# Attention feeding a mixture of experts: three steps instead of four between scores and values, and another order of the last slot

## The chip, the cores and the metric

The kernel runs on one core of a Trainium2 chip. The metric is the device time of one launch in microseconds (us), measured for the whole program. A profiled execution gives the trace that is quoted below; its times are counted from the start of its span. Engines are named as in the profile: PE is TensorE (PEld its weight loads), DVE is VectorE, ACT is ScalarE, POOL is GpSimd, SP is SyncE, which here only issues DMAs. Each engine runs its instructions in the order in which the program gives them to it.

## The reference

Inputs are `q`, `k`, `v` of 8 batches x 8 heads x 576 positions x 64, and `phi` of 8 x 8 x 576 x 32. Two stages follow one another, all in float32:

```
a    = softmax(phi, over the 32 memories)
k_m  = einsum('bhsm,bhsd->bhmd', a, k);  v_m likewise with v
x    = softmax(q @ k_m^T / 8) @ v_m              # per head, 32 scores a position
x    = x as 4608 tokens x 512
e    = argmax(x @ w_gate), gate = softmax(...)[e], eom = sigmoid(x @ w_output_gate)[e]
out  = gate * eom * (relu(x @ w1[e]) @ w2[e])    # 8 experts, 512 -> 1024 -> 512
```

So the keys and values are first condensed into 32 memories per head, every position attends to these, and each token of the result then goes through the two layers of one expert.

## The kernel before, in words

**Attention.** Batches are taken in four pairs. The positions of a pair are cut into five groups (four of 256 positions of one batch, and one of the 64 left over of both), which makes 20 groups, numbered here 0 to 19. For each pair, `memory` builds the condensed keys `kT_...` and values `ve_b` (transpositions of the softmaxed `ph`, sums over chunks `kvt` in L691, a closing matmul L697, scaling on ACT in L708, transpositions L717, copies to `kT` and `vT_b` in L722 and L723, and the small matmul L731). Each group then passes through these pieces:

- C, `scores` (L782, PE): 16 or 32 small matmuls into a PSUM tile `bpd`
- S, `shift`: a transposition out of `bpd` (L790, DVE), the row maximum (L793, DVE), its subtraction (L795, POOL)
- X, `expo`: the exponential (L799, ACT)
- D, `divide`: sum and reciprocal (L805, L807, L809, DVE), multiplication (L810, POOL)
- B, `back`: the transposition back to `aT` (L815, DVE)
- V0 and V1, `values` (L828, PE; the copy to `xo` L830, ACT); the group of leftovers has only V0. `store` then writes `xo` to the scratch tensor `xs` by a DMA on SP, and a deferred reduction `lg` (L947, DVE) collects the router's logits.

C, V0 and V1 take their `bpd` in rotation from two buffers.

**The table that orders it.** `attention` is a generator. Step t of its loop walks through the list `ORDER`, and the piece named there is done for group t minus its `LAG`. Between the pieces stand M and m (one step of `memory`) and R with a number (that many steps of the routing). After each pair `rank` computes the routing of its tokens; from the second pair on, `route_early` makes from it the expert of the first slots (`slot`) and the lists of tokens (`idx_ga`), after which POOL issues the indirect gathers `xg` (L483). While two pairs are done, routing runs at double pace.

**The opening.** Up to step `START` attention runs alone. At step `START - 1` the rest of `memory` is forced to its end. At step `START` the piece W splits the first two weight blocks into high and low halves (L521 on ACT, L522 on DVE), and after S the loop yields "open". From there the expert stage `run` leads: after each half unit of a slot it calls `hook`, which does three entries of `ORDER` and two routing steps.

**The expert stage.** The list `order` has 14 slots in the unconditional stream: ten of three blocks of 128 tokens, then four of two. `turn_x` transposes the gathered tokens (L993) and splits them into `xh` and `xl`; the first layer (L1127) multiplies each of four weight blocks in three passes (high by high, low by high, high by low), ACT and DVE make `hh` and `hl` of the result (L1132, L1133), and the second layer (L1146) goes through the weight blocks u = 4 to 7 with the blocks k of 128 tokens inside. When u is 7, `finish_y` scales a block's result on ACT (L1106) and POOL scatters it to `out` by an indirect DMA (L1107). Behind the stream stand slots of single blocks under a condition on a counted number (L1256); in the profiled execution none of them runs.

## Time and profile before

| quantity | value |
|---|---|
| median of 3 runs | 595.33 us (595.21 to 598.23) |
| the profiled execution's own time | 595.97 us |
| its span | 594.3 us |
| mean granted clock of TensorE | 0.959 |
| PE busy | 539.3 us (91%) |
| DVE, ACT, POOL busy | 340.9, 273.0, 160.7 us |
| DMA | 124.13 MB, mean 209 GB/s |

The page of the profile divides the span into 40 slices of some 15 us and gives the busy share of each engine by slice; the views of windows, of time order and of waits cut it finer. A busy PE is not a PE at its peak, and an engine's idle time counts only where others wait for it, so the shares are read by stage: attention alone up to about 115 us, the opening, the expert stage with the rest of attention between its matmuls up to about 190 us, the expert stage alone, and the end.

### The profile page before, as it was taken

Reading aid. Unit: us, or ns where it says so; the run is one execution under the profiler, and the core shown is the slowest. Engines: PE = TensorE matmul, PEld = TensorE weight load, DVE = VectorE, ACT = ScalarE, POOL = GpSimd, SP = SyncE. Lnnn points to the kernel's source line nnn. Section 1 sums busy time; section 2 is a strip of 40 time slices with the busy share of each in tenths; the row PEclk is TensorE's granted clock in tenths of the full one; section 3 lists DMA queues with packets and bytes.
Section 4 is the critical chain, followed back from the end, with each engine's and each line's share of the span. In section 5 each row is a group of like instructions: output and inputs, shape, how many; then the busy total and the mean of one; then the engine's idle time right before and its main releaser. Section 6 shows DMA issues by size and latency. Waiting matters only on the chain. (4 is left out here: it accounts for less than half of the span.)

```text
span 594.3 us, 10781 instructions
## 1 busy us (share of the span) xinstructions
PE 539.3 (91%) x4107; PEld 464.3 (78%) x4107; DVE 340.9 (57%) x686; ACT 273.0 (46%) x456; POOL 160.7 (27%) x192
## 2 busy tenths in 40 slices
PE   3788677788999999999999999999999999999980
PEld 2455455487788898998989899898989988989970
DVE  4487789677855589983544535354453526556200
ACT  4376554544445365434435444444444445555310
POOL 2244376731345036203303030130303012300100
PEclk9979879879999999999999999999999999999995
DMA  8999999974558578646646446474645538762000
GB/s 300 413 374 387 410 378 324 318 251 142 160 169 299 174 243 281 213 128 200 219 142 206 130 162 192 136 221 142 199 126 166 164 136 261 242 206 82 28 18 13
DMA packets 41276, 124.13 MB, mean 209 GB/s; under 512 B 9408, under 2 KB 9472, under 8 KB 40832
## 3 DMA queue, kind: packets, MB, share of 16 engines
q1 hardware_dynamic: 35136, 102.71, 52.2%
q0 software_dynamic: 6080, 20.65, 9.7%
q8 instruction: 34, 0.56, 0.4%
q14 instruction: 26, 0.21, 0.1%
HBM read 102.99 MB, written 20.87 MB: 208 GB/s over the span
## 5 line engine op out<-in xcount | busy, mean ns | idle before, releaser
L1127 PE MATMUL bps<-xh,whl 128*128 128x384 f32 (+1 forms) x896 | 213.8, 322 | 0.0
L1146 PE MATMUL bps<-whl,hh 128*128 128x512 f32 x608 | 203.7, 399 | 0.0
L522 DVE TENSOR_TENSOR whl<-w,whl 128x1024 fp32r<-128x1024 f32 x112 | 136.4, 1227 | 71.3 <-ACT whl L521 70.8
L1127 PEld LDWEIGHTS bps<-xh,whl 128*128 128x128 f32 x896 | 157.1, 190 | 1.4 <-issue 0.6
L1127 PE MATMUL bps<-xl,whl 128*128 128x384 f32 (+1 forms) x448 | 143.8, 321 | 0.0
L1146 PEld LDWEIGHTS bps<-whl,hh 128*128 128x128 f32 x608 | 114.2, 188 | 25.7 <-issue 2.5
L1146 PE MATMUL bps<-whl,hl 128*128 128x512 f32 x304 | 118.7, 390 | 0.0
L521 ACT CAST whl<-w 128x1024 fp32r<-128x1024 f32 x112 | 115.9, 1046 | 0.0
L1132 ACT ACTIVATE hh<-bps 128x384 fp32r<-128x384 f32 (+1 forms) x96 | 48.9, 510 | 102.0 <-PE bps L1127 97.7
L1133 DVE SCALAR_TENSOR_TENSOR hl<-bps,hh 128x384 fp32r<-128x384 f32 (+1 forms) x96 | 55.2, 576 | 58.9 <-ACT hh L1132 51.3
L1127 PEld LDWEIGHTS bps<-xl,whl 128*128 128x128 f32 x448 | 85.1, 190 | 0.5
L1107 POOL DMA_INDIRECT out<-y,idx_ol x23 | 23.1, 1003 | 213.7 <-ACT y L1106 186.4
L1146 PEld LDWEIGHTS bps<-whl,hl 128*128 128x128 f32 x304 | 57.3, 189 | 10.1
L995 DVE TENSOR_TENSOR xl<-bps,xh 128x384 fp32r<-128x384 f32 (+1 forms) x48 | 27.8, 579 | 60.7 <-ACT xh L994 60.5
L1106 ACT ACTIVATE y<-bps,xg 128x512 f32<-128x512 f32 x38 | 26.2, 689 | 68.9 <-issue 23.1
L994 ACT CAST xh<-bps 128x384 fp32r<-128x384 f32 (+1 forms) x48 | 23.9, 498 | 72.9 <-PE bps L993 71.2
L483 POOL DMA_INDIRECT xg<-xs,idx_gl x23 | 28.2, 1227 | 24.3 <-DVE idx_ol L242 17.6
L830 ACT COPY xo<-bpd 128x576 f32<-128x576 f32 x36 | 22.5, 639 | 22.5 <-PE bpd L828 13.1
L795 POOL TENSOR_TENSOR ea<-ea,mx 128x512 f32<-128x512 f32 (+1 forms) x20 | 19.2, 962 | 46.0 <-DVE mx L793 41.7
L828 PE MATMUL bpd<-ve_b,aT 64*128 64x144 f32 (+1 forms) x320 | 28.6, 327 | 2.1 <-DVE ea L790 1.9
L913 POOL TENSOR_SCALAR Aw<-iota_row,row 128x128 bf16<-128x128 bf16 x36 | 26.9, 763 | 12.4 <-DVE row L903 12.4
L993 PE MATMUL bps<-ident,xg 128*128 128x128 f32 x152 | 26.0, 286 | 2.3 <-DVE ea L790 1.8
(232 smaller groups left out, 427.1 us busy)
## 6 DMA issues: line engine op xcount, KB each, us to landing
w<-wall SPq DMA_DIRECT2D x112, 512.0 KB
kvt<-kv SPq DMA_DIRECT2D x32, 512.0 KB
xs<-xo SPq DMA_DIRECT2D x16, 576.0 KB
qt<-qT SPq DMA_DIRECT2D x16, 512.0 KB
ph<-phiT SPq DMA_DIRECT2D x3, 1152.0 KB
kv<-kv SPq DMA_DIRECT2D x4, 512.0 KB
ph<-phiT SPq DMA_DIRECT2D x4, 288.0 KB
xs<-xo SPq DMA_DIRECT2D x8, 144.0 KB
```

Source lines behind the costliest of these rows:

```text
L483: G.indirect_dma_start(out=z["xg"][:, k], out_offset=None, in_=xs[0:z["rows"]], in_offset=bass.IndirectOffsetOnAxis(ap=z["idx"][0][:, q:q ...
L521: A.copy(hl[:, 0], w[:])
L522: V.tensor_tensor(hl[:, 1], w[:], hl[:, 0].bitcast(F32), ALU.subtract)
L828: T.matmul(px[to:to + n, r, sl], z["aT"][h, o:o + n], ves[2 * bp + b][h, g], start=True, stop=True)
L913: (G if AWP else V).tensor_scalar(Aw[:, bp * NCH + c], iota_row[:], row[:, c:c + 1], None, ALU.is_equal)
L993: T.transpose(pt[:, j, k * P:(k + 1) * P], xg[:, k, o:o + P], ident[:])
L995: V.tensor_tensor(xl[:, c:c + w, 0:n], pt[:, :, 0:n], xh[:, c:c + w, 0:n].bitcast(F32), ALU.subtract)
L1106: A.activation(y[:], py, AF.Copy, scale=z["xg"][:, k, P:P + 1])
L1127: T.matmul(pb[:, j % pb.shape[1], 0:n_], w[:, b, o:o + P], x[a][:, cc, 0:n_], start=(n == 0), stop=(n == 11))
L1132: A.activation(h_[:, js, 0:n_], pb[:, :, 0:n_], AF.Relu)
L1133: V.scalar_tensor_tensor(l_[:, js, 0:n_], pb[:, :, 0:n_], 0.0, h_[:, js, 0:n_].bitcast(F32), ALU.max, ALU.subtract)
L1146: T.matmul(py[k], h[u - 4][a][:, f, k * P:(k + 1) * P], w[:, b, DM * f:DM * f + DM], start=(u == 4 and f == 0 and n == 0), stop=(u == 7 an ...
```

## The change

`ORDER` is rewritten and four numbers beside it are changed. X is now done in the step of its S (`LAG` 0 instead of 1), B one step behind S instead of two, and V two steps instead of three; D keeps its lag of one. V0 now stands behind D, X between V0 and V1, and B behind V1 near the end of the step. The list has 15 entries instead of 16 (R0, which did nothing, is gone). `START` is 16 instead of 17. In `several`, the second layer of the last slot of a stream goes through all four weight blocks for the first block of tokens and then again for the next, instead of through all blocks of tokens for each weight block; for all other slots the order of that layer is the same.

```diff
-ORDER = ["R4", "W", "X", "S", "R0", "m", "D", "M", "B", "V0", "R1", "R1", "V1", "M", "m", "C"]
-LAG = {"X": 1, "B": 2, "D": 1, "V": 3, "C": -1}
+ORDER = ["R4", "W", "S", "m", "D", "V0", "R1", "M", "X", "V1", "R1", "M", "B", "m", "C"]
+LAG = {"X": 0, "B": 1, "D": 1, "V": 2, "C": -1}
 TICK = 0
 HOOK = (3, 2)
-START = 17
+START = 16
@@ several @@
             py = [bank([DM], "ps") for _ in range(nb)]
-            for u in range(4, 8):
+
+            turns = [(u, k) for u in range(4, 8) for k in range(nb)]
+            if 8 * i + 8 == st.hi:
+                turns.sort(key=lambda t: t[1])
+            for step, (u, k) in enumerate(turns):
                 w = st.take(i, u)
-                for k in range(nb):
-                    for f in range(2):
-                        for n, (a, b) in enumerate(PASS):
-                            T.matmul(py[k], h[u - 4][a][:, f, k * P:(k + 1) * P], w[:, b, DM * f:DM * f + DM],
-                                     start=(u == 4 and f == 0 and n == 0), stop=(u == 7 and f == 1 and n == 2))
-                    if u == 7:
-                        finish_y(z, k, py[k])
-                    hook()
-                    step = nb * (u - 4) + k
-                    if step in TURN[nb]:
-                        nxt(TURN[nb].index(step))
-                st.done(PUMP[0])
+                for f in range(2):
+                    for n, (a, b) in enumerate(PASS):
+                        T.matmul(py[k], h[u - 4][a][:, f, k * P:(k + 1) * P], w[:, b, DM * f:DM * f + DM],
+                                 start=(u == 4 and f == 0 and n == 0), stop=(u == 7 and f == 1 and n == 2))
+                if u == 7:
+                    finish_y(z, k, py[k])
+                hook()
+                if step in TURN[nb]:
+                    nxt(TURN[nb].index(step))
+                if k == nb - 1:
+                    st.done(PUMP[0])
```

How the table moves instructions is seen at three places.

**POOL around the first gathers.** The three gathers `xg<-xs,idx_ga` are the first tokens of the expert stage. Before, POOL's order there is this (L795 is the subtraction of S, L810 the multiplication of D; the form 128x256 belongs to the leftover group 14):

```order
L795 TENSOR_TENSOR ea<-ea,mx 128x256
L810 TENSOR_TENSOR ea<-ea,sa 128x512
L483 DMA xg<-xs,idx_ga 128x576 x3
L795 TENSOR_TENSOR ea<-ea,mx 128x512
L810 TENSOR_TENSOR ea<-ea,sa 128x256
```

And now:

```order
L795 TENSOR_TENSOR ea<-ea,mx 128x512
L810 TENSOR_TENSOR ea<-ea,sa 128x512
L710 TENSOR_TENSOR ve_b<-kvm,hmask 128x2x128
L483 DMA xg<-xs,idx_ga 128x576 x3
L795 TENSOR_TENSOR ea<-ea,mx 128x256
L810 TENSOR_TENSOR ea<-ea,sa 128x512
```

The subtraction for group 14 stood ahead of the gathers and now stands behind them; ahead of them now stands that of group 13.

**ACT up to the opening.** Before, the last rows of ACT ahead of the expert stage are these (L722 with `kT_197` and `kT_198` are the condensed keys of the last pair's two batches, L799 the exponentials, L830 the copies of values, L708 the scaling of the memory, L521 the piece W):

```order
L722 COPY kT_197<-bpa 64x128 x2
L723 COPY vT_b<-bpa 64x256
L799 ACTIVATE ea<-ea 128x256
L830 COPY xo<-bpd 128x576 x2
L799 ACTIVATE ea<-ea 128x512
L708 ACTIVATE kvm<-pk,rs 128x128 x2
L722 COPY kT_198<-bpa 64x128 x2
L723 COPY vT_b<-bpa 64x256
L830 COPY xo<-bpd 128x576 x2
L521 CAST whl<-w 128x1024 x2
```

And now:

```order
L799 ACTIVATE ea<-ea 128x256
L830 COPY xo<-bpd 128x576
L722 COPY kT_197<-bpa 64x128 x2
L723 COPY vT_b<-bpa 64x256
L830 COPY xo<-bpd 128x576
L799 ACTIVATE ea<-ea 128x512
L830 COPY xo<-bpd 128x576
L708 ACTIVATE kvm<-pk,rs 128x128 x2
L722 COPY kT_198<-bpa 64x128 x2
L723 COPY vT_b<-bpa 64x256
L521 CAST whl<-w 128x1024 x2
```

The exponential of group 14 stood behind the copy to `kT_197` and now stands ahead of it; the exponential of group 15 now stands between the two copies of values of group 13.

**PE behind the first layer of the first slot.** L246 is the matmul that counts tokens for the next routing; it takes its operand `ohc_90` from DVE. Before:

```order
L828 MATMUL bpd<-ve_b,aT 128x144 x4
L246 LDWEIGHTS ones_b
L246 MATMUL pr<-ohc_90,ones_b 128x8
L1146 MATMUL bps<-whl,hh 128x512
L1146 MATMUL bps<-whl,hl 128x512
```

And now (L1149 is the line of before's L1146):

```order
L1149 MATMUL bps<-whl,hh 128x512 x2
L1149 MATMUL bps<-whl,hl 128x512
L1149 MATMUL bps<-whl,hh 128x512
L782 MATMUL bpd<-qt,kT_198 32x256 x8
L246 LDWEIGHTS ones_b
L246 MATMUL pr<-ohc_90,ones_b 128x8
```

Before, values stood directly ahead of L246; now six matmuls of the second layer and the scores of group 18 stand between the values and it.

## The prediction

> **What bounds the kernel now.** I read the page first (its slices), then windows of 5 us around the opening, then every engine in order of time there, and last the chain of waits.
>
> ```profile
> PE   3788677788999999999999999999999999999980
> ```
> ```profile
> 115.00:120.00 5.00, 3.67 (x51) 1.84 (x49) 3.38 (x7) 4.69 (x9) 2.15 (x3) 0.56 1.07 400
> 120.00:125.00 5.00, 4.02 (x16) 4.02 (x17) 4.03 (x8) 1.44 (x3) 2.76 (x3) 0.50 0.98 371
> ```
>
> In the slices PE has holes up to the tenth one (about 150 us) and is then full until the last two. So between the first slots and the end, only PE's own work counts, and neither edit takes a matmul away. What can move the end is when the first layer (L1127) starts, what stalls PE in the ten or twenty microseconds behind that, and what comes after the last matmul. The two windows (columns: PE, PEld, DVE, ACT, POOL busy, granted clock, DMA share, GB/s) are the opening.
>
> The end, from POOL, ACT and PE in order of time and from the chain of waits:
>
> ```profile
> 576.32 0.69 ACT L1106 ACTIVATE y<-bps,xg 128x512 f32<-128x512 f32 x1 [9.00 <-PE bps L1146]
> 577.28 0.97 POOL L1107 DMA_INDIRECT out<-y,idx_ol  x1 [17.93 <-ACT y L1106]
> 577.68 0.69 ACT L1106 ACTIVATE y<-bps,xg 128x512 f32<-128x512 f32 x1 [0.67 <-PEq L1257]
> 581.79 0.97 POOL L1107 DMA_INDIRECT out<-y,idx_ol  x1 [3.54 <-ACTq L1257]
> ```
> ```profile
> 577.28 3.74 DMA out<-y,idx_ol
> ```
>
> The second scatter of the last slot has its data at 577.68 + 0.69 = 578.37 but starts at 581.79: the chain shows that what ends last before it is the landing of the first scatter, at 577.28 + 3.74 = 581.02. Scatters to `out` go one after another.
>
> **The end of the program, costed.** Matmuls of the second layer follow one another at (576.98 - 576.30)/3 = 0.227 us:
>
> ```profile
> 576.30 0.39 PE L1146 MATMUL bps<-whl,hl 128*128 128x512 f32 x1
> 576.98 0.39 PE L1146 MATMUL bps<-whl,hl 128*128 128x512 f32 x1
> ```
>
> The last slot has two blocks of 24 such matmuls. With all of block 1 behind block 0, block 0 is complete 24 x 0.227 = 5.4 us before the end of PE instead of 1.36 us; its scatter starts at about 573.2 and lands by 577. The second then waits only for its own `y`. The first scatter started 0.27 us behind its `y` (577.01 to 577.28), which gives 578.64 and a gain of 3.15 us; with the 0.77 us that passed between release and start of the second (581.02 to 581.79) it is 2.65. I take **-3.0**. Nothing behind the last scatter changes. The weights of all four blocks must be split by then: the last L522 is long past (DVE's last start is at 552.6).
>
> ```profile
> 552.64 1.23 DVE L522 TENSOR_TENSOR whl<-w,whl 128x1024 fp32r<-128x1024 f32 x1 [0.26 <-ACT whl L521]
> ```
>
> The Trainium skill (DMA: Bandwidth & Descriptors, Anatomy of one DMA) fits a DMA issued from GpSimd as 2.0 us plus its bytes over 436 GB/s. For 256 KB that is an estimated 2.6 us, so the first scatter would have blocked only to 579.9 and the gain would be some 1.3 us. The row has 3.74 us, and it decides.
>
> **The opening, costed.** I set T at the first gather and follow the queues on both sides of it.
>
> ```profile
> 108.30 1.25 POOL L483 DMA_INDIRECT xg<-xs,idx_ga  x1 [1.40 <-DVE i L240]
> 112.18 1.06 POOL L795 TENSOR_TENSOR ea<-ea,mx 128x512 f32<-128x512 f32 x1
> 113.27 0.63 ACT L799 ACTIVATE ea<-ea 128x512 f32<-128x512 f32 x1 [3.08 <-POOL ea L795]
> 114.21 0.59 PE L717 MATMUL bpa<-ident,kvm 128*128 128x128 f32 x2 [2.40 <-ACT kvm L708]
> 114.83 0.53 ACT L722 COPY kT<-bpa 64x128 f32<-64x128 f32 x2 [0.42 <-PE bpa L717]
> 116.84 2.00 ACT L521 CAST whl<-w 128x1024 fp32r<-128x1024 f32 x2
> 120.98 2.18 PE L993 MATMUL bps<-ident,xg 128*128 128x128 f32 x9 [1.83 <-DVE ea L790]
> 122.81 0.67 PE L1127 MATMUL bps<-xh,whl 128*128 128x384 f32 x1
> ```
>
> Now: T = 108.30; three gathers hold POOL to 112.16; the exponential of group 15 waits for POOL; the memory's scaling, `kT_198` and the copies of values follow on ACT; the casts W start at T + 8.54; 5.97 us behind them comes L1127, at T + 14.51.
>
> Changed, by the order of ACT and POOL: the gathers end at T + 3.9. Behind them on POOL stands the subtraction of group 14 (0.61), on ACT its exponential (0.42), a copy of values (0.64), and only then `kT_197` (0.53): T + 6.1. The scores of group 15 need it and wait on PE; cold they take 1.11, to T + 7.2. Then S of 15 (0.71 + 0.69), its subtraction (1.05), its exponential (0.63), a copy of values (0.64) and half the scaling (0.3): T + 11.2. L717 0.59, `kT_198` 0.53, `vT_b` 0.37: the casts start at T + 12.7, and with 5.97 and one `lg` (0.3) L1127 comes at T + 19.0. That is **+4.5** from T. Durations that were not quoted yet, and the parts of S, D and B:
>
> ```profile
> 105.28 0.61 POOL L795 TENSOR_TENSOR ea<-ea,mx 128x256 f32<-128x256 f32 x1
> 106.27 0.42 ACT L799 ACTIVATE ea<-ea 128x256 f32<-128x256 f32 x1
> 116.47 1.11 PE L782 MATMUL bpd<-qt,kT 64*32 64x256 f32 x16
> 107.90 0.71 DVE L790 STREAM_TRANSPOSE ea<-bpd 128x512 f32<-128x512 f32 x1
> 108.64 0.69 DVE L793 TENSOR_REDUCE mx<-ea 128x16 f32<-128x512 f32 x1
> 114.58 0.68 DVE L805 TENSOR_REDUCE sa<-ea 128x16 f32<-128x512 f32 x1
> 115.29 0.32 DVE L807 TENSOR_TENSOR sa<-sa,eps 128x16 f32<-128x16 f32 x1
> 115.64 0.25 DVE L809 RECIPROCAL sa<-sa 128x16 f32<-128x16 f32 x1
> 144.57 0.65 DVE L815 STREAM_TRANSPOSE aT<-ea 128x512 f32<-128x512 f32 x1
> ```
>
> Its bounds: 0, if `kT_197` is copied before the gathers after all; +6, if every matmul on the way is cold.
>
> T itself comes earlier. The routing that makes the gathers' lists starts when the values of group 9 are out, and it needs as many routing steps as now. Values of group 9 move to the place where those of group 8 stand:
>
> ```profile
> 82.97 2.29 PE L828 MATMUL bpd<-ve_b,aT 64*128 64x144 f32 x16
> 88.69 0.72 PE L828 MATMUL bpd<-ve_b,aT 64*64 64x144 f32 x16
> 84.35 0.64 ACT L830 COPY xo<-bpd 128x576 f32<-128x576 f32 x1 [0.35 <-PE bpd L828]
> 89.50 0.64 ACT L830 COPY xo<-bpd 128x576 f32<-128x576 f32 x1
> ```
>
> Their copies stand 89.50 - 84.35 = 5.15 us apart, less one back transposition (0.65) that DVE must do earlier: **-4.5**. Bounds: -2.65 (if DVE alone sets the pace, what falls away before T is one S and one D, 0.71 + 0.69 + 0.68 + 0.32 + 0.25) and -5.7 (the two values, 88.69 - 82.97). So the opening's two terms cancel, with both ends at -5.7 and +3.4.
>
> In the Trainium skill (TensorE: Matmul & The Clock Gate, Part 1) an idle window of about 3.4 us halves PE's clock, and about as much work restores it. The granted clock of 0.50 from 120 us agrees. The wait for `kT_197` on PE is, by my sum, about 3 us, just under that window; by the page the scores of group 15 could be warm and the sum 0.45 less, or cold as I took them.
>
> SP's order also changes: the last two memory chunks `kvt`, 512 KB each, go out behind the first three weight blocks `w`, which SP issues ahead of T.
>
> ```profile
> w<-wall SPq DMA_DIRECT2D x112, 512.0 KB
> ```
>
> Together that is 2.6 MB, 6.4 us at the 400 GB/s of the window from 115. By my sum the chunks are used just ahead of the scaling, some 10 us behind T: covered. Without that cover, what they are late is added to the opening.
>
> **Behind the opening.** One group's scores more fall between the expert matmuls: (134.19 - 133.60) = **+0.6**.
>
> ```profile
> 133.60 0.66 PE L782 MATMUL bpd<-qt,kT 64*32 64x256 f32 x16
> 134.19 0.44 PE L1127 MATMUL bps<-xh,whl 128*128 128x384 f32 x1
> 144.99 0.76 PE L828 MATMUL bpd<-ve_b,aT 64*128 64x144 f32 x8
> 148.12 0.17 PE L246 MATMUL pr<-ohc,ones_b 128*128 128x8 bf16 x1 [2.36 <-DVE ohc L870]
> ```
> ```profile
> 142.82 0.49 ACT L1132 ACTIVATE hh<-bps 128x384 fp32r<-128x384 f32 x1 [1.44 <-PE bps L1127]
> 146.30 0.55 DVE L1133 SCALAR_TENSOR_TENSOR hl<-bps,hh 128x384 fp32r<-128x384 f32 x1
> ```
>
> L246 stalls PE by 2.36 us because DVE is late: it has `hh` at 143.31 and gets to `hl` at 146.30. In the changed order S of a group stands further ahead and one B behind L870, so about 2 us of DVE's work (0.71 + 0.69 + 0.65) leave this stretch, and L246 stands behind six more matmuls and one C (0.6). I leave a stall of 0.7: **-1.6**; bounds -2.36 and 0. The B moved there has its V0 two hooks later, which hides it.
>
> **Sum.** -3.0 + 4.5 - 4.5 + 0.6 - 1.6 = -4.0. The profiled execution took 595.97 us (span 594.3), so 592.0 for it; the median of the runs is 0.64 lower, which gives 591.3. I say **591.5**.
>
> **Rivals.**
>
> *The opening gains most of a step.* If the chain behind the gathers lengthens by 1 us and not by 4.5, the time is 588.0. For it: ACT now waits only 3.08 us for POOL there. Against it: the order on POOL and ACT, by which that wait now stands ahead of two groups' work.
>
> *The opening comes later and eats the gain of the end.* T gains only DVE's 2.65 us (1.85 less) and the chain is cold all through (+6, 1.5 more): 594.9. For it: between 95 and 100 DVE is busy 4.89 us of 5, so it may set the pace of the routing. Against it: what stands between values of group 9 and the gathers is the same work in both orders.
>
> ```profile
> 95.00:100.00 5.00, 3.62 (x81) 2.68 (x79) 4.89 (x31) 3.06 (x7) 2.33 (x4) 1.00 1.02 400
> ```
>
> *Slower: values wait for B.* Now a whole step lies between B and V0 of a group; changed, it is two hooks: 4.1 us in the first layer (twelve matmuls of 384 columns each, 0.227 x 384/512 = 0.17 us) and 2.7 in the second (six of 0.227). DVE was 143.31 to 146.30, 3 us, late. If it is later than two hooks for the six groups behind the opening, PE stalls at each V0; at 1.5 us each that is 591.5 + 9 = 600.5. It decides once DVE's lateness passes two hooks. Against it: DVE loses work in just that stretch.
>
> **How the numbers follow.** Forecast (589.5 to 593.5) 0.50; opening earlier (588) 0.20; opening later (594.9) 0.22; values stall (600.5) 0.08. A measurement of this kernel tells about 0.5% from no change, here 592.35 and 598.3. Two thirds of the forecast's chance and all of the early opening lie below: faster 0.54. The rest of the forecast and the late opening: same 0.38. Slower 0.08. The range is 587.5 to 595.5: it takes in the early and the late opening and leaves out the stalls.
>
> **What would show it.** Right: the last scatter starts 0.3 to 0.8 us behind its `y`; the first gather comes near 104 and the first L1127 near 123; `kT_197` is copied behind the gathers; L246 stalls under 1 us. Wrong: L1127 before 120 or behind 126, a V0 that waits for DVE between 125 and 190, or a last scatter that still waits for a DMA.

## The result, and the profile after

The changed kernel takes **601.66 us** (median of 6 runs, 600.02 to 603.19) beside 595.4 us for the kernel before (6 runs, 593.72 to 598.23). The ratio is 1.0101, 95% interval 1.0072 to 1.0129: the change makes it 6 us slower. The prediction was 591.5 us, range 587.5 to 595.5, with a chance of 0.08 on slower; it was wrong in direction. Among the runs of the experiments below one, of the end alone, took 952.39 us; its ratio leaves that run out, its median does not (593.54 us, without it 593.02).

The profiled execution of the changed kernel took 601.28 us, its span is 599.5 (before 595.97 and 594.3). The span divides at the same marks as the prediction's sum:

| stretch | before | after | forecast | measured |
|---|---|---|---|---|
| start to first gather (T) | 108.30 | 110.87 | -4.5 | +2.57 |
| T to first L1127 | 14.51 | 21.10 | +4.5 | +6.59 |
| first L1127 to PE's end | 454.78 | 453.42 | +0.6 - 1.6 | -1.36 |
| PE's end to the span's end | 16.71 | 14.11 | -3.0 | -2.60 |

Two of the four terms came as forecast. What is missing against the forecast lies ahead of the first L1127: 7.1 us ahead of T, and 2.1 between T and L1127.

The end, from PE, ACT and POOL of the changed kernel in order of time, and from its chain of waits:

```profile
580.03 0.69 ACT L1106 ACTIVATE y<-bps,xg 128x512 f32<-128x512 f32 x1 [4.92 <-PE bps L1149]
581.00 0.97 POOL L1107 DMA_INDIRECT out<-y,idx_ol  x1 [13.85 <-ACT y L1106]
585.00 0.39 PE L1149 MATMUL bps<-whl,hh 128*128 128x512 f32 x1
585.48 0.69 ACT L1106 ACTIVATE y<-bps,xg 128x512 f32<-128x512 f32 x1 [4.75 <-PE bps L1149]
586.93 0.97 POOL L1107 DMA_INDIRECT out<-y,idx_ol  x1 [4.96 <-ACT y L1106]
```
```profile
581.00 5.16 DMA out<-y,idx_ol
```

The second scatter now waits for its own `y` (585.48 + 0.69 = 586.17) and starts 0.76 us behind it. But the first one has only just landed: it took 5.16 us in place of the 3.74 before, to 581.00 + 5.16 = 586.16. The two waits end level, so nothing is left to gain there by an earlier `y` alone.

The opening, from POOL, ACT and PE of the changed kernel in order of time:

```profile
110.87 1.24 POOL L483 DMA_INDIRECT xg<-xs,idx_ga  x1 [1.46 <-DMA w<-wall]
115.40 0.42 ACT L799 ACTIVATE ea<-ea 128x256 f32<-128x256 f32 x1 [4.53 <-POOL ea L795]
116.24 0.54 ACT L722 COPY kT<-bpa 64x128 f32<-64x128 f32 x2
116.55 0.94 PE L782 MATMUL bpd<-qt,kT 64*32 64x256 f32 x16 [1.75 <-ACT kT L722]
121.51 0.64 ACT L830 COPY xo<-bpd 128x576 f32<-128x576 f32 x1 [4.34 <-DMA xs<-xo]
125.09 1.99 ACT L521 CAST whl<-w 128x1024 fp32r<-128x1024 f32 x2
129.53 2.79 PE L993 MATMUL bps<-ident,xg 128*128 128x128 f32 x12 [4.10 <-issue]
131.97 0.67 PE L1127 MATMUL bps<-xh,whl 128*128 128x384 f32 x1
```

`kT_197` is indeed copied behind the gathers, and the next scores wait for it. But a wait that the prediction does not have stands behind it: 4.34 us for a store (`xs<-xo`) that must land before its buffer is written again. Not all of it is loss. The scaling of the memory (L708), which comes three rows of ACT later and starts at 123.09, needs PE's sums, and PE ends them at 122.08 + 0.28 = 122.36:

```profile
122.08 0.28 PE L697 MATMUL pk<-zero 1*128 1x256 bf16 x1
```

By that the store costs the casts at most 0.73 us here, as long as PE's own row stays as it is.

What happens ahead of T shows first in one step, from the scores' transposition (S, L790) of group 9 to that of group 10. Before, from DVE, ACT and POOL:

```profile
70.24 0.43 DVE L790 STREAM_TRANSPOSE ea<-bpd 128x256 f32<-128x256 f32 x1
73.92 0.53 ACT L722 COPY kT<-bpa 64x128 f32<-64x128 f32 x2
74.86 0.42 ACT L799 ACTIVATE ea<-ea 128x256 f32<-128x256 f32 x1
75.02 5.29 POOL L913 TENSOR_SCALAR Aw<-iota_row,row 128x128 bf16<-128x128 bf16 x9 [1.33 <-DVE row L903]
75.29 0.70 DVE L790 STREAM_TRANSPOSE ea<-bpd 128x512 f32<-128x512 f32 x1
```

The same step in the changed kernel, from DVE, POOL, ACT and PE:

```profile
72.84 5.24 POOL L913 TENSOR_SCALAR Aw<-iota_row,row 128x128 bf16<-128x128 bf16 x9 [0.33 <-DVE row L903]
73.38 0.44 DVE L790 STREAM_TRANSPOSE ea<-bpd 128x256 f32<-128x256 f32 x1
78.05 0.60 POOL L795 TENSOR_TENSOR ea<-ea,mx 128x256 f32<-128x256 f32 x1
78.69 0.42 ACT L799 ACTIVATE ea<-ea 128x256 f32<-128x256 f32 x1 [3.61 <-POOL ea L795]
79.69 0.71 DVE L815 STREAM_TRANSPOSE aT<-ea 128x512 f32<-128x512 f32 x1 [3.06 <-POOL ea L810]
80.30 0.53 ACT L722 COPY kT<-bpa 64x128 f32<-64x128 f32 x2
80.60 1.38 PE L782 MATMUL bpd<-qt,kT 64*32 64x256 f32 x16 [2.58 <-ACT kT L722]
82.07 0.72 DVE L790 STREAM_TRANSPOSE ea<-bpd 128x512 f32<-128x512 f32 x1 [1.42 <-PE bpd L782]
```

In both kernels a routing gives POOL a burst of nine one-hot rows (L913), over 5 us long. Before, the exponential (L799) and `kT` of that step were all but done when it began, and S of group 10 followed 5.05 us behind that of group 9. Now the subtraction (L795) of group 9 stands behind the burst, its exponential waits in the same step, and behind that exponential on ACT stand the copies of `kT`, on which PE's next scores wait; on DVE, B (L815) waits for the multiplication behind that subtraction. The step takes 8.69 us. The waits of a whole execution, by the view of waits; before:

```profile
ACT ea L799 <- POOL ea L795: 7.1, 3, 3.1
PE bpd L782 <- ACT kT L722: 2.1, 4, 1.0
```

and changed (us in total, times, longest):

```profile
DVE aT L815 <- POOL ea L810: 17.0, 12, 4.1
ACT ea L799 <- POOL ea L795: 15.3, 11, 4.5
PE bpd L782 <- ACT kT L722: 5.1, 4, 2.6
```

B's waits for POOL are new altogether. I call the two waits the two hand-overs: an engine takes in one step what POOL makes in that same step.

One step tells too little, since a delay can move on into the next. In the kernel before, the burst shows later: an exponential waits 2.66 us for POOL at 81.36, and the step from group 11 to group 12 takes 7.5 us. So the table below has the three steps from S of group 9 to S of group 12 too: 16.4 us before (to 86.60) and 20.7 changed (to 94.11). First before, then changed:

```profile
86.60 0.72 DVE L790 STREAM_TRANSPOSE ea<-bpd 128x512 f32<-128x512 f32 x1 [0.74 <-PE bpd L782]
```
```profile
94.11 0.70 DVE L790 STREAM_TRANSPOSE ea<-bpd 128x512 f32<-128x512 f32 x1
```

### The profile page after: what moved, and what is told of

Same layout as the page of the kernel before. It is cut to its first block, busy times and chain, and to the rows that moved or that the text cites. A ratio compares the mean times of both kernels' runs of the same rounds, so it can differ in the third digit from the quotient of the medians.

```text
span 599.5 us, 10767 instructions
## 1 busy us (share of the span) xinstructions
PE 546.3 (91%) x4107; PEld 468.9 (78%) x4107; DVE 340.2 (57%) x686; ACT 271.6 (45%) x456; POOL 160.9 (27%) x192
## 5 line engine op out<-in xcount | busy, mean ns | idle before, releaser
L1127 PE MATMUL bps<-xh,whl 128*128 128x384 f32 (+1 forms) x896 | 214.1, 322 | 0.0
L1149 PE MATMUL bps<-whl,hh 128*128 128x512 f32 x608 | 203.8, 400 | 0.0
L1127 PEld LDWEIGHTS bps<-xh,whl 128*128 128x128 f32 x896 | 157.1, 190 | 1.6 <-ACT hh L1132 0.4
L1127 PE MATMUL bps<-xl,whl 128*128 128x384 f32 (+1 forms) x448 | 143.9, 321 | 0.0
L1149 PEld LDWEIGHTS bps<-whl,hh 128*128 128x128 f32 x608 | 114.3, 188 | 23.0
L1149 PE MATMUL bps<-whl,hl 128*128 128x512 f32 x304 | 118.8, 391 | 0.0
L521 ACT CAST whl<-w 128x1024 fp32r<-128x1024 f32 x112 | 115.9, 1046 | 0.0
L1127 PEld LDWEIGHTS bps<-xl,whl 128*128 128x128 f32 x448 | 85.1, 190 | 0.5
L1107 POOL DMA_INDIRECT out<-y,idx_ol x23 | 25.1, 1090 | 209.9 <-ACT y L1106 186.9
L1149 PEld LDWEIGHTS bps<-whl,hl 128*128 128x128 f32 x304 | 57.3, 189 | 10.1
L828 PE MATMUL bpd<-ve_b,aT 64*128 64x144 f32 (+1 forms) x320 | 31.5, 343 | 7.3 <-DVE aT L815 2.9
L795 POOL TENSOR_TENSOR ea<-ea,mx 128x512 f32<-128x512 f32 (+1 forms) x20 | 19.2, 961 | 69.8 <-DVE mx L793 51.9
L828 PEld LDWEIGHTS bpd<-ve_b,aT 64*128 64x128 f32 (+1 forms) x320 | 23.1, 204 | 15.8 <-issue 8.6
L830 ACT COPY xo<-bpd 128x576 f32<-128x576 f32 x36 | 22.8, 634 | 22.0 <-DMA xs<-xo 8.4
L993 PE MATMUL bps<-ident,xg 128*128 128x128 f32 x152 | 25.3, 285 | 4.1 <-issue 4.1
```

What stands on the lines that cost most here:

```text
L521: A.copy(hl[:, 0], w[:])
L828: T.matmul(px[to:to + n, r, sl], z["aT"][h, o:o + n], ves[2 * bp + b][h, g], start=True, stop=True)
L993: T.transpose(pt[:, j, k * P:(k + 1) * P], xg[:, k, o:o + P], ident[:])
L1107: G.indirect_dma_start(out=out, out_offset=bass.IndirectOffsetOnAxis(ap=z["idx"][1][:, z["q0"] + k:z["q0"] + k + 1], axis=0), in_=y[:], in ...
L1127: T.matmul(pb[:, j % pb.shape[1], 0:n_], w[:, b, o:o + P], x[a][:, cc, 0:n_], start=(n == 0), stop=(n == 11))
L1149: T.matmul(py[k], h[u - 4][a][:, f, k * P:(k + 1) * P], w[:, b, DM * f:DM * f + DM], start=(u == 4 and f == 0 and n == 0), stop=(u == 7 an ...
```

## The experiments

The runs were timed in five sets, each beside the kernel before on the same chip; its medians in the five sets lie between 595.51 and 596.48, so a difference of 1 us between kernels of two sets is no finding. The positions come from one profiled execution of each kernel, and the same order of work has its first gather at 110.87 in one kernel and 112.89 in another (the changed kernel, and the table alone), so less than 2 us between two profiles tells nothing by itself.

| kernel | time | ratio, 95% interval | S 9 to 10 | S 9 to 12 | first gather | first L1127 |
| --- | --- | --- | --- | --- | --- | --- |
| before | 595.4 |  | 5.1 | 16.4 | 108.3 | 122.8 |
| changed | 601.7 | 1.0101 (1.0072 to 1.0129) | 8.7 | 20.7 | 110.9 | 132.0 |
| end alone | 593.5 | 0.9963 (0.9945 to 0.9982) | 5.0 | 16.3 | 107.4 | 121.9 |
| table alone | 605.1 | 1.0152 (1.0131 to 1.0174) | 8.7 | 22.2 | 112.9 | 134.3 |
| opening alone | 603.4 | 1.0107 (1.0076 to 1.0138) | 5.1 | 15.9 | 107.8 | 121.3 |
| B in the next step | 624.8 | 1.0513 (1.0484 to 1.0542) | 10.0 | 25.0 | 122.7 | 146.7 |
| routing ahead of B | 602.8 | 1.0121 (1.0083 to 1.0160) | 8.9 | 21.1 | 111.0 | 132.7 |
| exponential in the next step | 599.0 | 1.0065 (1.0036 to 1.0094) | 7.2 | 20.0 | 109.3 | 130.2 |
| exponential behind the copies | 599.6 | 1.0066 (1.0051 to 1.0080) | 7.2 | 20.3 | 109.1 | 130.0 |
| multiplication on DVE | 603.6 | 1.0138 (1.0118 to 1.0157) | 9.0 | 20.7 | 112.9 | 135.1 |
| both hand-overs gone | 599.5 | 1.0062 (1.0047 to 1.0076) | 6.2 | 16.9 | 105.8 | 126.6 |
| one-hots on DVE | 597.7 | 1.0040 (1.0018 to 1.0062) | 4.8 | 16.2 | 107.8 | 128.7 |
| burst split | 598.6 | 1.0044 (1.0024 to 1.0064) | 6.3 | 17.7 | 110.1 | 130.9 |
| end and one-hots on DVE | 593.4 | 0.9961 (0.9946 to 0.9976) | 6.6 | 16.6 | 107.8 | 122.2 |
| store first | 602.3 | 1.0097 (1.0070 to 1.0123) | 8.7 | 21.4 | 111.8 | 133.1 |
| gathers later | 601.0 | 1.0094 (1.0073 to 1.0116) | 8.5 | 20.9 | 113.5 | 130.9 |
| store and gathers | 599.3 | 1.0064 (1.0041 to 1.0087) | 8.7 | 21.5 | 114.3 | 130.8 |
| these and one-hots on DVE | 596.3 | 1.0011 (0.9990 to 1.0032) | 4.8 | 16.2 | 110.8 | 128.1 |
| three mends | 598.6 | 1.0053 (1.0034 to 1.0072) | 5.4 | 16.8 | 110.5 | 125.9 |
| four mends | 597.5 | 1.0022 (1.0008 to 1.0036) | 5.4 | 16.8 | 111.7 | 126.3 |

### The change taken apart

The end alone is the kernel before with the new order of the last slot. The table alone is the changed kernel without it. The opening alone is the kernel before with

```diff
-START = 17
+START = 16
```

> The kernel before with the one edit at the end: the last slot's second layer block by block; table, lags and opening as before. Theory (the two edits add up; in the changed kernel the last scatter starts 0.76 us behind its y and 14.1 us pass from the end of PE to the end of the span, where it was 16.7): 2.65 us less than the kernel before, 592.7 beside 595.4, ratio 0.9955. Rival (the end's gain hangs on the opening, or the first scatter still blocks the second): no change, 595.4, ratio 1.000.

> The changed kernel without the edit at the end: values two steps behind scores, opening at step 16, last slot as in the kernel before. Theory (the whole loss is the table's): 601.7 + 2.65 = 604.3, ratio to the kernel before 1.015. Rival (the edit at the end costs something, the table less): 601.7 or lower, ratio 1.010 or below.

> The kernel before with START 16 alone: table and lags as before, last slot as before. Theory (an opening one step sooner costs nothing by itself; one exponential, two copies of values and one S leave the way between the gathers and the casts, some 2.5 us, and one group's scores more stand between the expert matmuls, 0.6): first gather near 108 as before, casts near 114.5, time 593 to 594.5, ratio 0.997. Rival (the sooner opening is the loss: it stretches the chain behind the gathers by 6 us as in the changed kernel): 598 to 601, ratio 1.005 to 1.010.

The end alone gives 2.2 us, the table alone costs 9.4 (605.1 against 595.7 in its set); their sum, 7.2, stands beside 6.3 for the whole change. So within the noise the edits add up, and the whole loss is the table's.

The opening alone was missed on both sides. The first L1127 comes 1.5 us earlier, as the theory had it, and the stall at L246 nearly goes (0.46 us), yet the time is 7 us longer. It is lost later. Windows of PE in that kernel (columns as in the prediction: PE, PEld, DVE, ACT, POOL, clock, DMA share, GB/s), and what PE waits for there:

```profile
190.00:195.00 5.00, 0.60 (x5) 0.18 (x1) 0.00 (x0) 0.64 (x1) 3.78 (x5) 0.73 0.93 326
194.18 0.45 PE L993 MATMUL bps<-ident,xg 128*128 128x128 f32 x1 [4.03 <-DMA xg<-xs,idx_gb]
```

The experts begin a step earlier, but the lists of the next slots (`idx_gb`) are done at 188.6, where the kernel before has them at 179.2; PE runs out of slots and waits 5.9 us in all for their gathers. I read this as the price of values that still stand three steps behind their scores; no run shows that by itself. If so, the earlier opening needs the values' earlier step, and neither half of the table can be judged alone.

### Which hand-over stretches the steps

First the two hand-overs one by one, as the first theory (B) and its rival (the exponential) had them:

```diff
 B in the next step, behind S
-ORDER = ["R4", "W", "S", "m", "D", "V0", ..., "M", "B", "m", "C"]
+ORDER = ["R4", "W", "S", "B", "m", "D", "V0", ..., "M", "m", "C"]
-LAG = {"X": 0, "B": 1, ...}
+LAG = {"X": 0, "B": 2, ...}
 exponential in the next step
-ORDER = ["R4", "W", "S", "m", ..., "M", "X", "V1", ...]
+ORDER = ["R4", "W", "X", "S", "m", ..., "M", "V1", ...]
-LAG = {"X": 0, ...}
+LAG = {"X": 1, ...}
 routing ahead of B
+ORDER = ["R4", "W", "B", "S", "m", "D", "V0", "R1", "M", "X", "V1", "R1", "M", "m", "C"]
+LAG = {"X": 0, "B": 2, ...}
```

> The changed kernel, but the back transposition (B) of a group is put into the next step, behind S and ahead of V0 of the same group; lag of the values 2, X at lag 0, opening at step 16. Theory (DVE's 11 waits for POOL's multiplication, 16.4 us up to 135 us, stretch the steps, so that the gathers start at 110.87 and not near 104): without these waits the gathers start near 104 to 106 and the time falls by 5 to 7 us, to 595 to 597. Rival (ACT's 11 waits for POOL's subtraction, 15.3 us, stretch them): DVE's waits move elsewhere, the gathers stay near 110 and the time is 600 to 602. Second rival (only the chain behind the gathers counts): the gathers come earlier, the time stays at 600 to 602.

> The changed kernel, but the exponential (X) of a group is put into the next step, ahead of S, as in the kernel before; B stays behind D of the same step, lag of the values 2, opening at step 16. Theory (DVE's waits for POOL's multiplication are the cause): DVE still waits some 16 us, and the time is 600 to 603. Rival (ACT's waits for POOL's subtraction, 15.3 us, are the cause): these waits fall away, the gathers start near 104 to 106, the time is 595 to 597.

> The changed kernel, but B of a group stands in the next step, behind the four routing steps and ahead of S; X at lag 0, values at lag 2, opening at 16. Theory (DVE's wait for POOL's multiplication at the end of each step holds up the routing that follows it and with it PE, 4.66 us at L246): DVE's waits for the multiplication before the first gather fall from 11.6 to under 6 us, PE's wait at L246 falls to 2 to 3 us, first gather 1 to 3 us earlier, time 598.5 to 601. Rival (B later makes the values wait, as in the run with B behind S): PE waits for B at the values, first gather later than 112, time over 604.

B in the next step costs 23 us more. The run does not test what it was made for: DVE's waits for POOL are gone, but with B behind S and ahead of V0 a ring closes over one step. PE's scores wait in its queue behind the values, these for B, B on DVE for S, and S for the scores (PE waits for B at V0 17 times, 37.6 us in all, 4.5 at the longest). With the routing ahead of B, DVE's waits for POOL before T fall from 11.6 to 6.1 us, just above what was expected, PE's wait at L246 from 4.66 to 3.46, and the time stays at 602.8: S waits 20.4 us for PE there, where it waited 16.9. So B's waits, where DVE shows them, are not the time that is lost; the theory of B alone falls. The exponential in the next step gains 2.7 us, half of what its theory asked, and not at the burst: from S of group 9 to S of group 12 it still takes 20.0 us.

Then the multiplication was put on DVE (B never waits for POOL), the exponential was left in its step but placed behind the copies of `kT` on ACT, and both hand-overs were taken away at once (exponential in the next step, multiplication on DVE):

```diff
 multiplication on DVE
-G.tensor_tensor(eav, eav, sa..., ALU.mult)
+V.tensor_tensor(eav, eav, sa..., ALU.mult)
 exponential behind the copies
-ORDER = [..., "R1", "M", "X", "V1", "R1", "M", "B", "m", "C"]
+ORDER = [..., "R1", "M", "V1", "R1", "M", "X", "B", "m", "C"]
```

> The changed kernel with the division's multiplication (L810) on DVE instead of POOL, so that B never waits for POOL. Theory (what costs is the hand-over to POOL and back within one step, not DVE's own work): DVE's 11.6 us of waits at B go away, some 0.7 us of work per group comes in their place, POOL's subtractions run 1 us earlier; first gather 1 to 4 us earlier than 110.9, time 597.5 to 600.5. Rival (DVE is simply full: its work sets the steps): first gather 112 to 116, time 603 to 607.

> The changed kernel with the exponential (X) of a group still in its own step, but behind that step's second memory piece, so that on ACT it stands behind the copies of kT and of the second values and not ahead of them. Theory (in the changed order an exponential that waits for POOL stands on ACT ahead of the copies of kT, on which the next scores wait on PE: 3.61 us and 2.58 us at group 9): PE's waits of scores for kT fall below 2.5 us from 5.1, S of groups 9 and 10 stand about 7 us apart and not 8.7 (B still waits there for POOL), first gather 1.5 to 3 us earlier than 110.9, time 598 to 600. Rival (B's wait for POOL holds the step just as long): S 8.5 us apart, first gather 110 or later, time 601 to 603.

> The changed kernel with the exponential in the next step ahead of S, and the division's multiplication on DVE: neither ACT nor DVE takes a result of POOL in the step that asks for it. Theory (each of the two hand-overs passes POOL's bursts on, so that one alone brings little: 2.7 us less with the exponential, 1.9 us more with the multiplication): S of groups 9 and 10 stand under 6.5 us apart, first gather at 106 to 108, time 595 to 598, in spite of 0.69 us more of DVE's work per group. Rival (DVE's own work sets the steps): first gather 110 or later, time 600 to 603.

With the multiplication on DVE the time and the first gather are the rival's, and DVE's own work may have its part in that; but the same step is 9.0 us long although B waits for nothing, and DVE itself stands idle in it. From POOL, ACT and PE of that kernel:

```profile
74.14 5.53 POOL L913 TENSOR_SCALAR Aw<-iota_row,row 128x128 bf16<-128x128 bf16 x9
80.29 0.42 ACT L799 ACTIVATE ea<-ea 128x256 f32<-128x256 f32 x1 [4.00 <-POOL ea L795]
81.90 0.53 ACT L722 COPY kT<-bpa 64x128 f32<-64x128 f32 x2
82.20 1.38 PE L782 MATMUL bpd<-qt,kT 64*32 64x256 f32 x16 [3.15 <-ACT kT L722]
```

The delay comes through the exponential and `kT`. With the exponential behind the copies that way is shut (PE's waits for `kT` fall from 5.1 to 1.6 us), and the step is still 7.2, because B waits for POOL. With both gone it is 6.2. The three steps show it more plainly: they take 20.0 and 20.3 us with the exponential's way shut, 20.7 with B's, and 16.9 only with both. The two hand-overs are two doors for one delay. In time, though, both together (599.5, between the ranges of the theory and of its rival) bring no more than the exponential alone (599.0). The multiplication adds 13 us of work to DVE (16 of 0.71 and 4 of 0.43), which may be why, but was not separated; and that kernel's profiled execution, at 596.8 us, was the fastest of its six, so its early first gather flatters it.

### The burst itself

> The changed kernel with the nine one-hot rows of a routing (Aw, L913) on DVE instead of POOL. Theory (POOL's two bursts of one-hots, 5.24 us from 72.8 and 5.67 us from 100.3, stand ahead of a subtraction and a multiplication, and DVE and ACT, which now take both in the same step, wait behind them: 3.06 us of B's wait at 79.7): S of groups 9 and 10 stand 6 us apart and not 8.7, the first gather comes 2 to 4 us earlier than 110.9, time 598 to 600. Rival (the steps are long for another reason; DVE gets nine instructions more per routing): first gather at 110 to 113, time 601 to 604.

> The changed kernel with the first routing's one-hot rows (L913 x9 on POOL) given out one by one, so that six of the nine stand behind the subtraction of group 9 and the multiplication of group 8 instead of ahead of them; no work is moved to another engine. Theory (the burst ahead of these two makes DVE wait 3.06 us at B and ACT at X in that step, and the values of group 9 and the routing behind them come later by as much): S of groups 9 and 10 stand 6 to 7 us apart and not 8.7, first gather 1.5 to 3 us earlier than 110.9, time 598.5 to 600.5. Rival (the gain with the one-hots on DVE came from the second burst, or from POOL having less to do): first gather 110 to 112, time 601 to 603.

> The kernel before with the end block by block and the one-hot rows on DVE instead of POOL; table and opening as before. It tells whether the 4 us that this gave in the changed kernel hang on the changed table. Theory (before, no engine takes POOL's results in the same step, so the bursts are covered): within 1 us of the end alone, 592.5 to 594.5. Rival (POOL's bursts cost in any order): 3 to 4 us less, 589.5 to 590.5.

The one-hots went to DVE by a switch that the kernel has; the split only lets other pieces of the step in between one-hots of the first routing:

```diff
 one-hots on DVE
-AWP = 1
+AWP = 0
 burst split
-                    if c % 3 == 2:
+                    if bp == 0 or c % 3 == 2:
                         yield
```

On DVE the one-hots bring 4.0 us. The split moves six of nine one-hots of a single burst behind the subtraction and the multiplication and takes no work from POOL; the step falls from 8.7 to 6.3, the three steps from 20.7 to 17.7 (16.2 with the one-hots on DVE), and the time by 3.1 us. From POOL and DVE of the split kernel:

```profile
75.36 1.78 POOL L913 TENSOR_SCALAR Aw<-iota_row,row 128x128 bf16<-128x128 bf16 x3 [0.33 <-DVE row L903]
75.90 0.44 DVE L790 STREAM_TRANSPOSE ea<-bpd 128x256 f32<-128x256 f32 x1
77.11 0.61 POOL L795 TENSOR_TENSOR ea<-ea,mx 128x256 f32<-128x256 f32 x1
78.12 1.05 POOL L810 TENSOR_TENSOR ea<-ea,sa 128x512 f32<-128x512 f32 x1 [0.40 <-DVE sa L809]
82.15 0.72 DVE L790 STREAM_TRANSPOSE ea<-bpd 128x512 f32<-128x512 f32 x1 [1.97 <-PE bpd L782]
```

Its first gather came only 0.8 us earlier and not 1.5 to 3, since S of groups 8 and 9 was already 2.5 us later in that execution than in the changed kernel's, ahead of the burst. In the table of before the one-hots on DVE bring nothing (593.4 beside 593.5 for the end alone). So the burst costs what it costs only because the changed table takes POOL's results in the step that makes them. This is shown by time and by the steps; the split was not run in the old table.

### The chain behind the gathers

> The changed kernel, but SP issues the first three weight blocks behind the two memory chunks and the store of the values of group 11, not ahead of them; every engine's own order is the same. Theory (that store is issued at 110.69 behind 2.6 MB and lands at 121.4; ACT waits 4.34 us for its buffer at the values of group 13, with the scaling of the memory and the casts behind it): the wait falls below 1 us, the casts start 3 to 4 us earlier behind the first gather (10 to 11 us, not 14.2), time 597.5 to 599.5. Rival (what comes next holds the chain, so the wait only moves): casts still 13 us or more behind the first gather, time 600.5 to 602.5.

> The changed kernel, but the three first gathers stand on POOL behind the subtraction of group 14 and the multiplication of group 13 and not ahead of them. Theory (the gathers hold POOL 3.9 us ahead of the chain subtraction, exponential, kT_197, scores, casts, while their own data has 8 us of slack before the casts are through): the gathers start 1.5 to 2 us later, but the casts 2.5 to 3.9 us earlier (121.2 to 122.6 in place of 125.1), time 598 to 599.5. Rival (something else, the store's buffer or the memory's last chunks, ends last in that chain): casts within 1 us of 125, time 600.5 to 602.5.

> The changed kernel with both orders changed that alone moved little: the store of group 11's values ahead of the first weight blocks on SP, and the first gathers behind the subtraction of group 14 and the multiplication of group 13 on POOL. Theory (two waits end at nearly the same time in the chain behind the gathers, the store's buffer at 120.5 and the subtraction's chain at 120.2, so only both together shorten it): casts at 120.5 to 122 in place of 125.1, first L1127 near 128, time 597.5 to 599. Rival (a third wait, the memory's last chunks, holds the casts): casts at 123.5 or later, time 600 to 602.

> The same as the run with store and gathers, and the one-hots on DVE. Theory (the bursts delay the first gather, the two orders shorten the chain behind it; the two add up): 4 us below the run with store and gathers, 593.5 to 595, so the changed table with these three comes level with the kernel before or just below it, but not below the end alone (593.5). Rival (the chain is then held by the memory, which no mend moves): 597 to 598, as with the one-hots alone.

The first run holds back the fetch of the first weight blocks, so that SP issues memory chunks and store ahead of them; the second holds back the gathers on POOL:

```diff
 store first
-                stream.fetch()
+                defer("wf", stream.fetch)    # LATE["wf"] = 10
 gathers later
-                gathers(0)
+                defer("ga", lambda: gathers(0))    # LATE["ga"] = 5
```

On SP of the changed kernel (its DMA issues in order of time) the store of group 11's values stands behind three weight blocks and two memory chunks, 2.6 MB, and it lands at 121.4:

```profile
107.28 1.47 SPq L510 DMA_DIRECT2D w<-wall  x3
108.79 1.79 SPq L604 DMA_DIRECT2D kvt<-kv  x2
110.69 0.38 SPq L939 DMA_DIRECT2D xs<-xo  x1
```

Store first takes ACT's wait of 4.34 us away, but the casts come as late as before: ACT's next copies and exponential then wait for PE and POOL instead, and the scaling behind them waits 0.80 us for PE's sums (L697). Gathers later moves `kT_197` from 116.24 to 114.36, and then the store's wait (5.17 us) ends at 120.46. Measured from S of group 14, since these runs move the gathers themselves, the casts come 14.8 us later in the changed kernel, 15.0 with the store first, 13.9 with the gathers later, and 12.9 with both. In time: 0.6 us more, 0.7 less, and 2.4 less with both. The first two are within the noise, and the interval with both (1.0041 to 1.0087) still overlaps the changed kernel's. So the runs point to two waits that end there at nearly the same time, and do not prove it. With both, the casts come at 123.9 and not by 122, as the rival of a third wait had it: the scaling waits 0.55 us for PE's sums there too. With the one-hots on DVE 3.0 us more fall away, and the time is 596.3, between the range of the theory and the rival's: level with the kernel before (1.0011, interval 0.9990 to 1.0032).

> The changed kernel with three mends at once: exponential in the next step ahead of S (alone: 2.7 us less), one-hots on DVE (alone: 4.0 us less), first gathers behind the subtraction of group 14 and the multiplication of group 13. Theory (the three causes are different waits): 601.7 - 2.7 - 4.0 - 3 = 592.0, first gather near 107.5, first L1127 near 123. Rival (exponential and one-hots cure the same wait): 594.5 to 596.

> The changed kernel with exponentials behind the copies, one-hots on DVE, the store of group 11's values ahead of the weight blocks, and the first gathers behind the subtraction of group 14 and the multiplication of group 13. Theory (every known wait of the opening is gone, and the opening is a step sooner as was meant): first L1127 at 124 to 126, time 592 to 594.5, level with the end alone (593.5). Rival (the exponential and the one-hots cure the same wait): 595 to 597, as with the three orders (596.3).

Three mends (exponential in the next step, one-hots on DVE, gathers later) and four (exponential behind the copies, one-hots on DVE, store first, gathers later) have the first L1127 at 125.9 and 126.3, 6 us earlier than the changed kernel but 4 us behind the end alone, and are still 4 to 5 us above the end alone. Both miss the theory's number and lie above the rival's too. Behind the opening they lose a part of what they gained: from the first L1127 to PE's end they take 456.7 and 456.0 us, the changed kernel 453.4. Values now wait there for DVE and ACT. From PE with three and with four mends:

```profile
164.44 0.76 PE L828 MATMUL bpd<-ve_b,aT 64*128 64x144 f32 x8 [1.31 <-DVE ea L790]
```

```profile
179.39 0.76 PE L828 MATMUL bpd<-ve_b,aT 64*128 64x144 f32 x8 [1.20 <-ACT xo L830]
```

Of the 445 us from 130 to 575 PE is idle 3.1 and 2.1 us in these two, and 0.1 in the changed kernel. No version with the new table beat the end alone. The best are the end alone, 593.5 us, and the end with one-hots on DVE, 593.4: 2.2 us below the kernel before and 8 below the changed one.

## Why the prediction was wrong, point by point

**The end, -3.0.** Right: -2.60 in the span and 2.2 in the times. The second scatter starts 0.76 us behind its `y`, which was the lower bound (2.65). That nothing else holds it is partly luck: the sum let the first scatter land 3.74 us behind its start, it took 5.16, and it landed 0.01 us ahead of the second `y`. The Trainium skill (DMA: Bandwidth & Descriptors, Anatomy of one DMA) by its fit for the first scatter would have made the gain 1.3 us; the measured gain lies with the row's 3.74 us. Scatters of the slots ahead landed in 2.61 us (558.38, before) and 2.62 (566.18, changed), as the fit has it; those of the last slot's first block took longer.

**T, -4.5.** This is the step that failed: +2.57, 7.1 us off and outside its bounds (-2.65 to -5.7). It rested on two claims. The first was that the copies of group 9's values take the place of group 8's, 4.5 us earlier. They come 1.0 us earlier, at 88.53 in place of 89.50:

```profile
88.53 0.64 ACT L830 COPY xo<-bpd 128x576 f32<-128x576 f32 x1
91.20 0.71 DVE L815 STREAM_TRANSPOSE aT<-ea 128x512 f32<-128x512 f32 x1 [1.29 <-POOL ea L810]
93.85 0.16 DVE L870 TENSOR_TENSOR ohc<-ohc,oc 128x8 bf16<-128x8 bf16 x1
94.06 0.17 PE L246 MATMUL pr<-ohc,ones_b 128*128 128x8 bf16 x1 [4.66 <-DVE ohc L870]
```

The spacing of 5.15 us was read from the kernel before, whose steps do not hold the hand-overs. The second claim was that the same work stands between these values and the gathers in both orders. A B with its wait for POOL now stands there on DVE ahead of the routing: L870 comes 5.3 us behind the copy (88.53 to 93.85) where it came 3.0 behind it (89.50 to 92.50), PE stands at L246 for 4.66 us, and its scores behind it wait too. From there to T it took 1.2 us more (17.0 in place of 15.8). L870 before, from DVE:

```profile
92.50 0.16 DVE L870 TENSOR_TENSOR ohc<-ohc,oc 128x8 bf16<-128x8 bf16 x1
```

Against the forecast the 7.1 us divide into four. S of group 9 comes at 73.38 in place of 70.24, 3.1 us late. From it to the copy it takes 15.2 us, 0.4 more than forecast (89.50 - 4.5 - 70.24 = 14.8). Then come 2.3 from the copy to L870 and 1.2 from there to T.

The first part is not the burst's, which begins only at 72.84. It is no chance of one profile: five kernels with the same order up to there (changed, table alone, store first, gathers later, store and gathers) have S of group 9 at 73.1 to 73.5, the four with the old table at 69.5 to 71.2. With the exponential in the next step it comes at 71.3, and from there to T takes 38.0 us, where the changed kernel has 37.5: what that run gains it gains ahead of the burst. What costs the rest of the 3.1 us stays open.

The second part is small, and yet the burst costs some 4 us there: with the one-hots on DVE that stretch takes 11.2 us, and with the burst split 12.7. The forecast did not notice because the old steps from which its spacing was read hold a long one too (7.5 us from group 11 to 12).

In time the burst's part is shown (3 to 4 us, by two runs and the control in the old table); the exponential's place has 2.0 to 2.7 us, and in the runs with both it did not add to the burst's. What B's wait ahead of the routing costs was not separated: the two runs made for it put another wait in its place.

The prediction had the mechanism in hand at one place. It saw that behind the gathers a subtraction, an exponential and then `kT_197` stand in line. It did not ask at which other steps POOL is busy long enough to do the same; the one-hots stand in none of its rows. The added wait that it did price, values waiting for B, never came: between 125 and 190 us no V0 of the changed kernel waits for DVE.

**The chain behind T, +4.5.** Right in kind, too small: +6.6, above its bound of +6, which was set without a sum. As far as the scores of group 15 it was right: `kT_197` is through at T + 5.9 (forecast 6.1), the scores at T + 6.6 (7.2). The Trainium skill (TensorE: Matmul & The Clock Gate, Part 1) would have the clock kept through an idle stretch shorter than its window. PE waited 1.75 us; the granted clock was 1.00 from 115 to 117 and the 16 matmuls took 0.94 us, but from 118 to 121 it was 0.50 all the same. So the trace does not bear the rule out as the prediction used it, and the 0.50 from 120 us in the kernel before was no agreement either: PE's longest wait ahead of it was 2.40 us.

From the scores to the casts it took 7.6 us and not 5.5. The sum had neither the store nor PE's own row between them; at the clock of 0.50 eight matmuls of values (L828) took 1.33 us, at 1.00 they take 0.76. How the 2.1 us divide between these stays open; the store has at most 0.73 of them, as above. From the casts to L1127 it took 6.9 us and not 6.3: all twelve transpositions (L993, 2.79 us) stood behind S there, and before only nine (2.18 us).

**SP's order.** The prediction said that the two memory chunks behind the first weight blocks are covered. They are; the store behind them is not. Every transfer behind the moved ones should have been followed, not only those that the move names. Alone it costs little, by the run with the store first; whether it does together with the gathers' place, the run with both suggests and does not prove.

**Behind the opening, +0.6 - 1.6.** Right: -1.36. L246 no longer waits there (155.79, where it had waited 2.36 us).

**Rivals and range.** The opening that comes later (594.9) had the right place, but priced the loss of T's gain and no more; that T could come later than before was excluded by a sentence, "the same work in both orders", and not by a row. The slower rival was put behind the opening, where PE in fact loses nothing.

## What to carry to other kernels

A consumer that is moved into the step that makes its data turns every long stay of the producer's queue into a stall of its own engine, and of all that stands behind it there: go through all steps for what else the producer's engine does (here one burst of 5 us per routing), not only through the step that the argument is about. The spacing of two rows of the old order is no price for a step of the new one. A delay should be measured over several steps, since one that leaves a step can come back in the next: here the exponential's place shortened one step by 1.5 us and three steps by 0.7. And two waits that end together, as the store and the gathers seem to here, each look harmless when mended alone; mend both before calling one innocent.

## What the runs showed of the hardware

A small DVE instruction can last as long as POOL is busy. In the kernel before, L641 on 128x4 took 2.80 us, from 80.70 to 83.50, while POOL ran a chain of instructions without a gap to 83.48; its other three take 0.11, 0.17 and 1.03 us, and in the changed kernel all four 0.17 at most. From DVE and the last of POOL's chain, before:

```profile
80.70 2.80 DVE L641 TENSOR_SCALAR rs<-ssum 128x4 f32<-128x4 f32 x1
82.87 0.61 POOL L710 TENSOR_TENSOR ve_b<-kvm,hmask 128x256 f32<-128x256 f32 x1
```

The Trainium skill (SBUF — State Buffer, SBUF: two separate sides) has DVE and GpSimd share one pair of ports that a GpSimd instruction holds for its whole length against some of DVE's; the rows agree with that, and here DVE's instruction came through only behind four of POOL's in a row. The changed order, in which DVE's sum follows S directly, lies more often beside POOL's subtraction: the median of L807 goes from 0.176 to 0.326 us. In all of L807 that is 2 us more, while L641 takes 3.5 less. The sum hides something, though: three instructions of the routing that makes the gathers' lists lie beside POOL's in the changed kernel and are stretched, L264 from 0.16 to 0.97 us, L297 from 0.18 to 0.91 and L215 from 0.35 to 1.07. The last two, from DVE of the changed kernel:

```profile
106.13 0.91 DVE L297 TENSOR_TENSOR q<-q,q 128x18 f32<-128x18 f32 x1
107.07 1.07 DVE L215 TENSOR_TENSOR eq<-iota_blk,q 128x108 bf16<-128x108 bf16 x1
```

POOL runs its subtraction and multiplication from 105.95 to 108.00 without a gap. These two stand right ahead of T; behind them PE waits 0.46 us for their result (L227 for L219), so they may have a part in the 1.2 us from L870 to T. No run separates that. A one-hot row of 128x128 took 0.58 us on POOL (5.24 for nine) and 0.17 on DVE (1.55 for nine, with the one-hots on DVE).
